# Softmax division in one VectorE piece, row-wise loads for four heads, shared masks, interleaved last products: attention and two gated MLPs on one core

## The chip, the cores and the metric

The kernel runs on one core of a Trainium2 chip. The metric is the device time of one execution, in microseconds (us). Engines are named as in the profile: PE is TensorE, DVE is VectorE, ACT is ScalarE, POOL is GpSimd, SP is SyncE, which here issues every DMA.

## What is computed

Three layers follow each other, all in float32. `q`, `k`, `v` are [4, 8, 576, 64] (batch, head, position, depth).

```python
scores = scale * np.matmul(q, k.transpose(0, 1, 3, 2))
rel = pos[:, None] - pos[None, :]
mask_plain = (rel >= 0) & (rel < 32)
mask_dil = (rel >= 0) & (rel < 128) & (rel % 4 == 0)
# heads 0..3 use mask_plain, heads 4..7 mask_dil
scores = np.where(masks[None], scores, -1e9)
attn = np.exp(scores - np.max(scores, axis=-1, keepdims=True))
attn = attn / (np.sum(attn, axis=-1, keepdims=True) + 1e-9)
x = np.matmul(attn, v)                       # then rows of 512: 2304 x 512
# first MLP: rms norm, then
xn = x / np.sqrt(np.mean(x * x, -1, keepdims=True) + 1e-6) * rms_g
g = xn @ w_gate
y = (g * sigmoid(g) * (xn @ w_val)) @ w_out  # 512 -> 1536 -> 512
# second MLP
out = (sigmoid(y @ w2_gate) * (y @ w2_val)) @ w2_out
```

## The kernel before

**Attention.** Two heads make a pair `hp` (0 and 1 plain, 2 and 3 dilated), so that 128 partitions are full. Both masks leave a window of 96 keys for 64 queries (the dilated heads are sorted by position modulo 4 first), so a pair of one batch is nine blocks, in three groups of three. There are 4 x 4 x 3 = 48 groups. `attn_group` makes one: 12 small score matmuls on PE (L982), mask and row maximum on DVE (L994, three instructions), `exp` with its sum on ACT (L1000, three), `sum + 1e-9` and reciprocal on DVE (L1007, L1008), the division as three multiplications (L1013 on POOL, by choice of the planner L1017 on DVE), three transposes on PE (L1027), their eviction on ACT (L1032), 12 value matmuls on PE (L1040), and an eviction into `xT` (L1052, L1060).

**How q and k come in.** Batch 0 goes through `first_qk`: whole rows of 256 bytes are loaded (L797) and PE turns them (L834, four operations of four transposes for a pair). The other twelve pairs go through `attn_load`: eight DMAs of 128-byte runs into `kraw` and `qraw` (L941), which have one buffer each, and two 32x32 transposes on DVE (L955). Values come through `values_of` (L894 for dilated pairs, L904 and L912 for plain ones), those of batch 0's dilated heads through `first_v` (into `xT`).

**First MLP.** The 2304 rows are six chunks `c` of 384. `x_norm(c)` squares `xT` on ACT (L1090), adds the four 128-row blocks on POOL for c > 0 (L1098, three additions), sums over partitions on PE (L1106), makes 1/sqrt by Newton steps (on DVE for c = 0; on POOL for c > 0, L1140 to L1144), spreads it (L1147, L1163), scales (L1186) and splits each value into a high and a low fp32r part (ACT or DVE L599/L601, POOL L603 or DVE L606). `mlp_step` then runs 12 + 12 matmuls of 384 columns (L1401) and `y_group` 12 more (L1481) for each of 12 blocks `f` of the hidden size; pass 0 takes `f` 0 to 5 for all chunks, pass 1 the rest. Chunk 0 needs ten groups of batch 0; chunk 1 needs ten more: two of batch 0, six of batch 1's dilated pairs and one of each of its plain pairs. The weights come as 64-bit words, are packed on ACT and DVE (L567 to L576) and split in the same way.

**Second MLP.** It works on blocks in seven products instead of eight (`unit`, `half`, L1709; `y_products`, L1632): a product is six matmuls of 288 columns, three for each of two `u`. Its input for a `u` is `hop`, seven high and low pairs, the last made by DVE, ACT and POOL after the last L1709 product. `y_products` gives 14 closures: seven for output half n = 0, then seven for n = 1. They are handed out between the products of the next `unit`; those of the last batch have no next `unit` and run in a row at the end, followed by transposes and stores (L1662, L1667, L1674).

**Order.** `Line` is a list scheduler that runs while the program is built: every `add` gives an operation an engine (or several to choose from), an estimated cost, what it reads and writes, its tiles and a due time. `emit` always takes the operation that can begin first; among operations that wait for a busy engine the smallest due time wins. An alternative engine has a penalty from `PARAMS`. Every engine's program, SP's DMA issues too, is in the order that this leaves. PE's products of the second MLP keep the order in which they were added (key `PE order`).

Of the kernel before, what the change touches and what calls it, by code (L numbers as in the profile page):

```python
# [8 lines left out]
F32 = mybir.dt.float32  # L9
# [6 lines left out]
NEG = -1.0e30  # L16
# [9 lines left out]
    "late": 0, "fill_share": -1.497, "fill_max": 6, "gather": 1.257, "w0_hi": 12.903,  # L26
    "w0_lo": 18.633, "h0_hi": 0.97, "h0_lo": -0.008, "x0_hi": 0.055, "x0_lo": 0.49, "ahead": 2,
    "todo0": 261.292, "todo1": 2.598, "todo2": 1.388, "todo3": 21.487, "xb_zero": 1.369,
    "stay": 0.055, "phase": 1.6, "fill_from": 6.083, "fill_gap": -7.771, "margin": 894.801,
    "wait": 1.635, "w_sq": 1.999, "w_hi": 1.306, "w_lo": 0.0, "x_hi": 5.948, "x_lo": 0.127,  # L30
    "h_hi": 13.236, "h_lo": 0.0, "qk": 0.148, "norm": 0.496, "pts": 11.821, "o": 0.0,
    "snap": 2.101, "h_ahead": 10.497, "h2_ahead": 7.278, "evac": 4.529, "holds": (6, 6),
    "norm_act": 8.92, "slack": 0.0, "share_v": 0.6, "share_p": 0.33, "cold": 1.7, "low": 0,
    "high": 0.39, "recip": 0.3, "rel1": 72.061, "span1": -5.933, "rel2": 16.991, "span2": 0.874,
    "ys": 0.545, "ts": 14.649, "cross": 0.06, "same": 0.04, "dma_lat": 1.7, "dma_rate": 330000.0,
# [3 lines left out]
    "ld_b": -50.429, "ld_v": -48.262, "ld_c": -52.06, "ld_d": -2.674, "lead": -0.197,  # L39
    "xdue": 16.042, "wdue": -1.702, "wslope": 2.797, "wload": -154.451, "wload_step": -3.584,  # L40
    "warm_n": 36, "warm_t": -0.367, "warm_dt": -0.481, "warm_c": 19, "warm_m": 5,
    "warm_late": -1.242, "warm_due": 26.914, "mask_cost": 0.18, "exp_cost": 0.36, "s_cost": 0.546,
# [302 lines left out]
def attention_then_two_gated_mlps(  # L345
# [145 lines left out]
    def build_masks(kinds, due):  # L491

        base = masks["p1"][:, 0]

# [1498 lines left out]
```

## Time and profile before

| | us |
|---|---|
| median of 3 runs | 1003.61 (1000.10 to 1006.71) |
| the profiled execution | 1002.46 |
| its span, first to last instruction | 1000.7 |

The profiled execution has 1.8 us outside its span. The profile gives the busy time of each engine, the granted clock of PE as a share of its full 2.4 GHz, the chain of work that ended last, groups of instructions by line, and what each engine waited for. In rows by stretch the figures are the stretch, its length, then busy us of each engine with the number of its instructions in brackets. A busy PE is busy at its granted clock, so a stretch at 0.7 holds less work than one at 1.0.

### The profile page before, as it was taken

How to read it: one execution, taken by the hardware profiler on the slowest of the kernel's cores; microseconds unless marked ns; L12 is line 12 of the kernel's file. 1: busy time of each engine (PE TensorE's matmuls, PEld its weight loads, DVE VectorE, ACT ScalarE, POOL GpSimd, SP SyncE). 2: the span in 40 equal slices, each digit the busy share in tenths (PEclk: the TensorE clock that was granted, in tenths of full speed). 3: DMA queues.
4: the chain of work that ended last, by engine and by line, in shares of the span. 5: the costliest groups of instructions: out<-in, count | busy, mean ns of one | idle time of the engine just before them, and what ended most of it. 6: DMA issues, size and time to landing. Idle time of an engine off the chain costs nothing.

```text
span 1000.7 us, 20034 instructions
## 1 busy us (share of the span) xinstructions
PE 974.8 (97%) x7096; PEld 943.4 (94%) x7096; DVE 709.3 (71%) x1699; ACT 485.9 (49%) x1336; POOL 332.8 (33%) x512
## 2 busy tenths in 40 slices
PE   7989899999999999999999999999999999999997
PEld 6768799999999999999999999999999999999996
DVE  5687997776884877641322579778987689887775
ACT  5875656664432643322222355657673446444432
POOL 4556865443540100002220124445440017441210
PEclk8779799999999999999999999999999999999999
DMA  9949788594887688965654355545275464548633
GB/s 195 183 102 224 161 222 233 154 250 147 274 297 266 212 302 257 342 217 189 221 197 141 108 168 185 208 170 194 83 270 183 162 221 148 173 143 239 178 81 75
DMA packets 213252, 194.53 MB, mean 194 GB/s; under 512 B 137312, under 2 KB 178848, under 8 KB 213152
## 3 DMA queue, kind: packets, MB, share of 16 engines
q1 hardware_dynamic: 213152, 193.25, 63.1%
q8 instruction: 56, 0.92, 0.4%
q14 instruction: 44, 0.36, 0.1%
HBM read 129.50 MB, written 63.70 MB: 193 GB/s over the span
## 4 chain that ended last, share of the span: by engine, by line
PE 87%; DVE 4%; DMA 3%; SPq 2%; ACT 1%; POOL 1%; issue 1%; ACTq 0%; DVEq 0%; POOLq 0%
PE g L1401 14%; PE y L1481 14%; PE v L1401 14%; PE y L1632 13%; PE att L1709 11%; PE v L1709 5%; PE y L1709 5%; PE g L1709 4%; PE att L982 3%; PE att L1040 2%; SPq L797 1%; DMA xT<-in_v_dram 1%; PE att L1027 1%; DMA out_dram<-ob 1%; PE y L1040 0%
## 5 line engine op out<-in xcount | busy, mean ns | idle before, releaser
L1401 PE MATMUL g<-xo,w 128*128 128x384 f32 x864 | 166.6, 340 | 0.4 <-POOL xo L603 0.4
L1481 PE MATMUL y<-h,wo 128*128 128x384 f32 x864 | 166.4, 338 | 0.0
L1401 PE MATMUL v<-xo,w 128*128 128x384 f32 x864 | 163.3, 336 | 0.7 <-DVE t L1449 0.7
L1401 PEld LDWEIGHTS g<-xo,w 128*128 128x128 f32 x864 | 152.5, 191 | 1.7 <-POOL xo L603 1.0
L1401 PEld LDWEIGHTS v<-xo,w 128*128 128x128 f32 x864 | 149.9, 188 | 2.2 <-DVE t L1449 1.1
L1481 PEld LDWEIGHTS y<-h,wo 128*128 128x128 f32 x864 | 149.5, 188 | 1.4
L599 ACT CAST h<-t 128x384 fp32r<-128x384 f32 (+1 forms) x140 | 66.2, 475 | 103.0 <-DVE t L1449 83.7
L1449 DVE TENSOR_TENSOR t<-t,v 128x384 f32<-128x384 f32 x72 | 39.5, 549 | 82.8 <-PE v L1401 77.8
L603 POOL TENSOR_TENSOR h<-t,h 128x288 fp32r<-128x288 f32 (+1 forms) x45 | 43.6, 970 | 153.1 <-ACT h L599 149.7
L1581 DVE SCALAR_TENSOR_TENSOR pt<-y,pt 128x288 f32<-128x288 f32 x133 | 59.8, 451 | 29.5 <-PE y L1632 28.5
L606 DVE TENSOR_TENSOR h<-t,h 128x384 fp32r<-128x384 f32 (+1 forms) x95 | 56.6, 598 | 24.7 <-ACT h L599 23.5
L1632 PE MATMUL y<-h,wo 128*128 128x288 f32 x399 | 72.1, 295 | 0.3 <-ACT h L599 0.2
L1735 ACT ACTIVATE t<-t 128x288 f32<-128x288 f32 x72 | 31.9, 444 | 73.1 <-DVE t L1726 73.0
L1013 POOL TENSOR_SCALAR pr<-pr,rs 128x96 f32<-128x96 f32 x134 | 51.0, 395 | 46.8 <-DVE rs L1008 37.2
L567 ACT ACTIVATE wz<-wst 128x512 f32<-128x512 f32 x72 | 47.8, 669 | 32.6 <-DMA z<-wz 21.1
L1632 PEld LDWEIGHTS y<-h,wo 128*128 128x128 f32 x399 | 59.3, 188 | 1.1 <-ACT h L599 0.5
L1000 ACT ACTIVATE pr<-pr,nmx 128x96 f32<-128x96 f32 x144 | 52.2, 365 | 12.9 <-DVE nmx L994 12.7
L603 POOL TENSOR_TENSOR w<-wz,w 128x256 fp32r<-128x256 f32 x40 | 32.9, 831 | 73.7 <-ACT w L599 73.7
L576 DVE SCALAR_TENSOR_TENSOR wz<-wst,wz 128x512 int32<-128x512 int32 x72 | 54.7, 763 | 0.8
L570 DVE TENSOR_SCALAR wz<-wz 128x512 int32<-128x512 int32 x72 | 35.2, 493 | 26.8 <-ACT wz L567 25.9
L573 DVE SCALAR_TENSOR_TENSOR wz<-wst,wz 128x512 int32<-128x512 int32 x72 | 53.2, 742 | 1.1
L1270 DVE TENSOR_TENSOR t<-t,t 128x288 f32<-128x288 f32 x82 | 49.7, 608 | 4.2 <-POOL x L603 1.2
(220 smaller groups left out, 2019.9 us busy)
## 6 DMA issues: line engine op xcount, KB each, us to landing
z<-wz SPq DMA_DIRECT2D x54, 256.0 KB, 5.7
xo<-xs SPq DMA_DIRECT2D x23, 576.0 KB, 5.8
wst<-in_moe_w_gate_dram SPq DMA_DIRECT2D x24, 512.0 KB, 6.5
wst<-in_moe_w_val_dram SPq DMA_DIRECT2D x24, 512.0 KB, 5.0
wst<-in_moe_w_out_dram SPq DMA_DIRECT2D x24, 512.0 KB, 6.3
xs<-xs SPq DMA_DIRECT2D x21, 576.0 KB, 2.9
wst<-xs SPq DMA_DIRECT2D x18, 576.0 KB, 4.2
x<-xo SPq DMA_DIRECT2D x24, 384.0 KB, 4.5
```

The source lines that it names most:

```text
L573: add("DVE", Shared(0.595), lambda: nc.vector.scalar_tensor_tensor(out=z.t, in0=top(), scalar=-0x80000000, in1=z.t, op0=ALU.bitwise_and, o ...
L576: add("DVE", Shared(0.595), lambda: nc.vector.scalar_tensor_tensor(out=z.t, in0=low(), scalar=29, in1=z.t, op0=ALU.logical_shift_right, op ...
L599: add("ACT", act(n), lambda: nc.scalar.copy(out=hi(), in_=src()), reads=reads, writes=[key] + [order] * bool(order), tiles=tiles + [dst], ...
L603: add("PL", pool(n), lambda: nc.gpsimd.tensor_tensor(out=lo(), in0=src(), in1=hi().bitcast(F32), op=ALU.subtract), reads=reads, writes=[ke ...
L606: other=(kind + "_lo", "DVE", dves(n), lambda: nc.vector.tensor_tensor(out=lo(), in0=src(), in1=hi().bitcast(F32), op=ALU.subtract)))
L1000: add("ACT", PARAMS["exp_cost"], lambda u=u: nc.scalar.activation(out=pr.t[:, u], in_=pr.t[:, u], func=ACTF.Exp, bias=nmx.t[:, u:u + 1], s ...
L1013: add("PL", Shared(0.305), lambda u=u: nc.gpsimd.tensor_scalar(out=pr.t[:, u], in0=pr.t[:, u], scalar1=rs.t[:, u:u + 1], scalar2=1.0, op0= ...
L1401: nc.tensor.matmul(out=bank.t, lhsT=w[:, l, cols], rhs=x, start=kk == order[0] and n == 0, stop=kk == order[-1] and n == 2)
L1481: nc.tensor.matmul(out=yb.t, lhsT=w.t[:, l, s], rhs=hs[r].t if broad(p, c) else hs[r].t[:, r], start=n == 0 and j == 0, stop=n == HOLDS[p] ...
L1581: add("DVE", dve(T), lambda: nc.vector.scalar_tensor_tensor(out=t.t[:, e, h], in0=bank.t, scalar=0.5, in1=t.t[:, e, h], op0=ALU.mult, op1= ...
L1632: nc.tensor.matmul(out=bank.t, lhsT=w.t[:, u, a, n], rhs=hs[u].t[:, d], start=first and u == 0 and m == 0, stop=u == NF // 2 - 1 and m == ...
L1709: nc.tensor.matmul(out=bank.t, lhsT=l.t[:, a, cols], rhs=r.t[:, d, j], start=first and j == 0 and m == 0, stop=j == 1 and m == 2, skip_gro ...
```

## The change

- **Division.** With `fuse` 99 every group takes the new branch: `divided` issues `sum + 1e-9`, the reciprocal and the three multiplications as one operation on DVE. POOL and ACT have no part in it. (`whole_norm` is 0, so that branch is not built.)
- **Whole rows.** `by_pe` is 2: the first two pairs of batch 1 that are met, its dilated pairs (1, 2) and (1, 3), use `first_qk` with `start=False`, staged in the ring `xo` of four buffers, and PE turns them; their values still come through `values_of`. (`few` is 0: `dilated_values` is not used.)
- **Masks.** Five masks of three blocks become six masks of one block, by bound.
- **Row sums.** With `early_sum` the additions for c > 0 run into block 2, in the order 3, 0, 1, and may run on DVE.
- **Last products.** With `mixed` the 14 closures of the last batch run in the order 0, 7, 1, 8, 2, 3, ... 13; the banks are kept by half and name.
- **Due times and penalties.** Nearly all numbers of `PARAMS` are others. `fast` 1 leaves the Newton steps of c > 0 on POOL as they were. `packed` stays 0.

```diff
-    "high": 0.39, "recip": 0.3, "rel1": 72.061, "span1": -5.933, "rel2": 16.991, "span2": 0.874,
+    "wait": 1.628, "w_sq": 0.142, "w_hi": 10.229, "w_lo": 0.083, "x_hi": 16.209, "x_lo": 0.682,
...
-    "hi3": 58.56, "lo4": 66.519, "hi4": 99.279, "lo5": 125.255, "hi5": 121.604, "ld_a": -59.069,
-    "ld_b": -50.429, "ld_v": -48.262, "ld_c": -52.06, "ld_d": -2.674, "lead": -0.197,
+    "lo4": 75.925, "hi4": 97.447, "lo5": 103.804, "hi5": 68.022, "ld_a": -47.059, "ld_b": -40.139,
+    "ld_v": -42.85, "ld_c": -37.834, "ld_d": -2.595, "lead": 0.175, "xdue": 11.352, "wdue": 2.621,
...
+    "pk": -0.353, "pk_act": -0.974, "pk_pl": 12.322, "few": 0, "sg": -4.518, "early_sum": 1,
+    "sq_add": 0.555, "xdue1": 0.715, "fast": 1, "fuse": 99, "mixed": 1, "whole_norm": 0,
...
-        add("PL", 1.0, band, writes=["band"], due=due)
-        for n, (key, bounds) in enumerate(kinds):
...
+        add("PL", 1.0, band, writes=[("mask", None)], due=due)
+        for n, b in enumerate((0, 16, 32, 48, -16)):
+            m = masks[b]
+            add("DVE", 0.2, lambda m=m: nc.vector.tensor_copy(out=m, in_=base),
+                reads=[("mask", None)], writes=[("mask", b)], due=due + n)
...
+        def divided():
+            recip()
+            for u in range(G):
+                nc.vector.tensor_scalar(
+                    out=pr.t[:, u], in0=pr.t[:, u], scalar1=rs.t[:, u:u + 1], scalar2=None,
+                    op0=ALU.mult)
+
+        if n < PARAMS["fuse"]:
+            add("DVE", Shared(PARAMS["recip"] + 0.34), divided, writes=[("e", gk, u) for u in range(G)],
+                tiles=[pr, rs], due=due + 1.25)
...
+        into = KK_FIRST[0] if PARAMS["early_sum"] else 0
         if c:
-            for kk in range(1, KD):
+            for kk in KK_FIRST[1:] if into else range(1, KD):
                 add("PL", pool(T1), lambda kk=kk: nc.gpsimd.tensor_tensor(
-                    out=sq.t[:, 0], in0=sq.t[:, 0], in1=sq.t[:, kk], op=ALU.add),
-                    reads=[x for x in keys if x[2] == kk], writes=[x for x in keys if x[2] == 0],
-                    tiles=[sq], due=due)
+                    out=sq.t[:, into], in0=sq.t[:, into], in1=sq.t[:, kk], op=ALU.add),
+                    reads=[x for x in keys if x[2] == kk], writes=[x for x in keys if x[2] == into],
+                    tiles=[sq], due=due, other=("sq_add", "DVE", dves(T1),
+                    lambda kk=kk: nc.vector.tensor_tensor(
+                    out=sq.t[:, into], in0=sq.t[:, into], in1=sq.t[:, kk], op=ALU.add)))
...
-                        banks[key] = new("ps", tag, [P, T], F32, 2 if tag == "att" else 1)
+                        banks[n, key] = new("ps", tag, [P, T], F32, 2 if tag == "att" else 1)
...
-                    first_qk(*g[:2], (("at", "kraw", RAWS), ("at", "qraw", RAWS)), at, at, False)
+                    home = (("sb", "xo", NX),) * 2
+                    first_qk(*g[:2], home, at, at, False)
...
+        if PARAMS["mixed"]:
+            extra = [extra[i] for i in (0, 7, 1, 8, 2, 3, 4, 5, 6, 9, 10, 11, 12, 13)]
         for _, fn in extra:
             at += fn(at)
```

## Rows read from the trace of the kernel before

**Rows 1.** Busy us by stretch: length, PE, PEld, DVE, ACT, POOL; clock; DMA share, GB/s

```profile
11.60:30.00 18.40, 14.53 (x149) 11.59 (x149) 12.34 (x61) 13.29 (x52) 8.69 (x19) 0.71 0.99 197
30.00:45.00 15.00, 14.94 (x169) 12.02 (x171) 8.09 (x40) 11.68 (x41) 6.62 (x19) 0.68 1.06 179
45.00:61.40 16.40, 12.36 (x142) 9.07 (x137) 14.01 (x71) 12.87 (x50) 6.58 (x18) 0.76 0.55 138
61.40:111.80 50.40, 48.86 (x430) 42.50 (x429) 40.55 (x123) 34.88 (x122) 35.94 (x59) 0.94 0.75 175
111.80:125.30 13.50, 10.79 (x86) 9.42 (x86) 12.78 (x43) 8.04 (x29) 11.29 (x25) 0.62 0.68 152
125.30:280.00 154.70, 154.40 (x1298) 143.76 (x1297) 120.68 (x353) 88.23 (x276) 78.90 (x156) 1.00 0.77 214
280.00:979.40 699.40, 697.49 (x4706) 695.68 (x4705) 483.49 (x974) 308.77 (x756) 175.53 (x187) 1.00 0.59 198
979.40:1000.70 21.30, 14.38 (x97) 12.55 (x95) 11.27 (x26) 4.11 (x10) 2.39 (x3) 0.96 0.27 57
```

**Rows 2.** Chain of waits, 62 to 150 us: start, us, what, instructions

```profile
95.00 0.64 PE att L982 x12
95.65 0.50 PE att L1040 x12
...
100.30 0.33 PE att L1027 x3
...
103.55 2.08 PE g L1401 x12
```

**Rows 3.** Timeline of PE, 0 to 140 us: start, us, what, shapes, count

```profile
109.50 2.33 PE L1481 MATMUL y<-h,wo 128*128 128x384 f32 x12
...
121.39 4.01 PE L1401 MATMUL g<-xo,w 128*128 128x384 f32 x12
```

**Rows 4.** Groups of PE instructions, 111.7 to 125.3 us: count, busy us, mean ns

```profile
L982 PE MATMUL att<-kT,qT 64*64 64x96 f32 x36 | 3.4, 368 | 0.5 <-DVE ms L1122 0.5
L1040 PE MATMUL att<-pts,v 96*64 96x64 f32 x24 | 1.5, 276 | 0.0
```

**Rows 5.** Timeline of SP's queue, 0 to 120 us: start, us, what, count

```profile
35.45 3.49 SPq L941 DMA_DIRECT2D kraw<-in_k_dram  x4
...
82.36 5.02 SPq L941 DMA_DIRECT2D kraw<-in_k_dram  x4
```

**Rows 6.** Timeline of POOL, 0 to 125 us

```profile
5.56 0.28 POOL L524 MEMSET mask_p<- 64x32 f32 x2
...
102.99 1.14 POOL L1013 TENSOR_SCALAR pr<-pr,rs 128x96 f32<-128x96 f32 x3
...
107.98 2.38 POOL L1098 TENSOR_TENSOR pt<-pt 128x384 f32<-128x384 f32 x2
...
111.75 1.45 POOL L1098 TENSOR_TENSOR pt<-pt 128x384 f32<-128x384 f32 x1
```

**Rows 7.** Chain of waits, 0 to 62 us

```profile
40.05 0.25 PE y L834 x4
```

**Rows 8.** Groups of DVE instructions, 60 to 120 us

```profile
L570 DVE TENSOR_SCALAR wz<-wz 128x512 int32<-128x512 int32 x10 | 5.9, 596 | 3.0 <-ACT wz L567 3.0
...
L1007 DVE TENSOR_SCALAR rs<-rs 128x3 f32<-128x3 f32 x12 | 3.3, 274 | 1.2 <-ACT pr L1000 1.2
```

**Rows 9.** Groups of DVE instructions, 120 to 280 us

```profile
L1007 DVE TENSOR_SCALAR rs<-rs 128x3 f32<-128x3 f32 x23 | 5.1, 221 | 4.1 <-ACT pr L1000 4.1
...
L1017 DVE TENSOR_SCALAR pr<-pr,rs 128x96 f32<-128x96 f32 x7 | 1.9, 282 | 0.2
```

**Rows 10.** Chain of waits, 960 to 1001 us

```profile
978.63 0.81 PE y L1709 x6
...
984.35 2.22 PE y L1632 x14
...
991.45 2.42 PE y L1632 x18
```

More of the change, by code (lines that the diff above doesn't have):

```diff
@@ L25 @@
 PARAMS = {
[L26 to L31, printed above, removed]
@@ L47 @@
-    "turns": 2, "raw0": 0, "sign": 1, "packed": 0, "pk": 0.869, "pk_act": -1.179, "pk_pl": 4.504,
-    "sg": 0.0,
+    "late": 0, "fill_share": -1.979, "fill_max": 6, "gather": 1.675, "w0_hi": 28.354,
+    "w0_lo": 12.639, "h0_hi": 9.993, "h0_lo": 0.526, "x0_hi": 0.211, "x0_lo": 1.621, "ahead": 2,
+    "todo0": 152.278, "todo1": 1.414, "todo2": -1.035, "todo3": 8.412, "xb_zero": -89.067,
+    "stay": 0.59, "phase": 1.6, "fill_from": 12.103, "fill_gap": -6.912, "margin": 510.725,
+    "wait": 1.628, "w_sq": 0.142, "w_hi": 10.229, "w_lo": 0.083, "x_hi": 16.209, "x_lo": 0.682,
@@ new lines @@
+    "h_hi": 10.394, "h_lo": 0.089, "qk": 0.068, "norm": 1.75, "pts": 12.096, "o": 0.661,
+    "snap": 1.157, "h_ahead": 31.842, "h2_ahead": 36.261, "evac": -0.905, "holds": (6, 6),
+    "norm_act": 24.671, "slack": 0.0, "share_v": 0.6, "share_p": 0.33, "cold": 1.7, "low": 0,
+    "high": 0.39, "recip": 0.3, "rel1": 46.586, "span1": -52.882, "rel2": 28.252, "span2": 0.857,
+    "ys": 4.918, "ts": 11.109, "cross": 0.06, "same": 0.04, "dma_lat": 1.7, "dma_rate": 330000.0,
[3 rows of a table added]
+    "ld_v": -42.85, "ld_c": -37.834, "ld_d": -2.595, "lead": 0.175, "xdue": 11.352, "wdue": 2.621,
@@ L489, in constants, with build_masks @@
             writes=["gam"], due=-4)
-    def build_masks(kinds, due):
-        base = masks["p1"][:, 0]
+    def build_masks(due):
+        base = masks[None]
         def band():
@@ L895, in dilated_windows @@
                     out=vt.t[p0:p0 + n, j], in_=vr[r, t0:t0 + n]),
-                    rows(n * n_heads, 4 * D), writes=[key], tiles=[vt], due=due + 0.12 * j)
+                    rows(n * n_heads, 4 * D), writes=[key], tiles=[vt], due=due + 0.12 * j, cost=0.58)
                 vkeys[j].append(key)
@@ L918, in plain_windows, with dilated_values @@
         return vkeys
-    def values_of(b, hp, due):
+    def dilated_values(b, due):
+        vt = new("at", "vd", [WIN, NB, HP, D], F32, 1)
+        pad = ("v pad", b, HP // 2)
+        add("PL", 0.3, lambda: nc.gpsimd.memset(vt.t[0:32, 0], 0.0), writes=[pad], tiles=[vt],
+            due=due)
+        vkeys = dilated_windows(vt, b, HP, HP, due)
+        vkeys[0].append(pad)
+        return vt, vkeys
+    together = {}
+    def values_of(b, hp, due):
+        if hp >= HP // 2 and PARAMS["few"]:
+            if b not in together:
+                together[b] = dilated_values(b, due)
+            vt, vkeys = together[b]
+            heads[b, hp] += (vt, 2 * hp - HP, vkeys)
+            return
         vt = new("at", "v", [WIN, NB, 2, D])
@@ L1108, in sums @@
                                  stop=last and t == TT - 1)
-        order = [0] if c else KK_FIRST
+        order = [into] if c else KK_FIRST
         for n, kk in enumerate(order):
```

105 lines of the change are left out of this document (52 added, 53 removed), and 4 rows, old and new, of the table PARAMS.

## The prediction, made before the changed kernel was run

> **What bounds the kernel now.** I read the page first (busy time, the 40 slices, the chain that ended last), then busy time by stretch, then for each stretch that loses time the chain of waits and the timelines of the engines in it. From 280 to 979.4 us PE is busy for 697.49 of 699.40 us at a granted clock of 1.00, which is the full 2.4 GHz, and from 125.3 to 280 for 154.40 of 154.70 [rows 1]. Nothing that this change does to DVE, ACT or POOL can shorten those 854 us; it can only lengthen them. What can be won lies in three places.
>
> *The front*, to 61.4 us, where chunk 0's first MLP product starts. From 11.6 us, when the first q and k have landed, PE is busy for 14.53 + 14.94 + 12.36 = 41.8 of 49.8 us, at 0.68 to 0.76 of the clock, a mix of its two levels, 1.2 and 2.4 GHz, and to 45 us the DMA engines are as good as full (0.99 and 1.06) [rows 1].
>
> *The gate of chunk 1.* Chunk 0's last product block starts at 109.50 and takes 2.33; the first of chunk 1 starts at 121.39 [rows 3]. In these 9.6 us PE does attention only: 36 score matmuls and 24 value matmuls [rows 4], at the full clock 3 x 0.64 and 2 x 0.50, and three transposes, 0.33, together 3.25 us [rows 2]. So 6.3 us are lost, and the clock falls to 0.62 over the stretch [rows 1]: the first block of chunk 1 takes 4.01 us instead of 2.08 [rows 2, 3], 1.9 more. That is 8.2 us.
>
> *The end.* The last product of the last unit ends at 979.44. The 14 products behind it are 84 matmuls; a run of 18 takes 2.42 us, so they are 11.3 us of work, and they end at 993.87, 14.4 us later [rows 10]. 3.1 us are lost, all before 984.35: from there PE runs without a wait, 71 matmuls in 9.5 us, so that only 13, or 1.7 us, were done in the 4.9 us before. PE waited for the high and low parts of the last `hop`.
>
> **The change part by part.** *Whole rows.* Today four pairs of batch 1 pass one after the other through the single `kraw` and `qraw`, from the first load at 35.45 to the fourth at 82.36 [rows 5]: three steps of 15.6 us. The first two pairs leave this line, so the two plain pairs that chunk 1 also waits for can be loaded some 31 us earlier, and so can every pair behind them. SP issues two DMAs of q and k for such a pair instead of eight; the weights queued behind them go out sooner. In exchange PE turns them: eight operations of 0.25 [rows 7], 2.0 us. They cost nothing if they fall into the 4.0 us that PE idles between 45 and 61.4 [rows 1], and 2.0 if not; I take 1.0. Their eight evictions replace four DVE transposes and go to ACT, which has 3.5 us free there and 15.5 in the next stretch [rows 1]: nothing. With that cover gone they are at most 8 x 0.6 = 4.8 us of ACT, priced by the widest elementwise DVE row [rows 8]. There is one new wait: the staging ring `xo` also holds chunk 0's normed input, whose transposes of the root (L1163) cannot be issued until these rows are turned, and all MLP products stand behind them on PE. Their turns take 2.0 us and have the whole front, so between 0 and 2 us; I take 0.
>
> *Early row sums.* At the gate POOL adds from 107.98 to 113.20: two additions of 1.19, other work, and the third [rows 6]. In the new order two of the three need no block of the plain pairs that comes last, so one of 1.19 is left: 4.0 us less before the 8.2 us of row sums, Newton steps and spread that follow until 121.39 and that stay as they are.
>
> *The division.* At the gate the three multiplications hold POOL for 1.14 us [rows 6]; three on DVE are 3 x 0.28 = 0.85 [rows 9], without a queue behind POOL's splits: 0.3 us or more for each group.
>
> Together these three move chunk 1's normed input by far more than the 9.6 us that it is late; the load is then not what comes last, but the scores, DVE and ACT of ten groups. I take 7.0 of the 8.2 us, since the row sums and the spread of the root (a few small matmuls with no row at the full clock) remain: between 0 and 8.2. What is late next? The later chunks ask for their groups at the same distance as before and lose 0.3 us today in 155 [rows 1], with their loads 31 us less early. I see no second gate.
>
> *DVE's load.* From 60 us on 35 groups pass [rows 8, 9], 105 multiplications; 7 are on DVE already [rows 9], so 98 x 0.282 = 27.6 us come to it. Between 61.4 and 280 it is busy for 40.55 + 12.78 + 120.68 = 174.0 of 218.6 us [rows 1]; it would be 201.6, in 211.6 us if the gate's 7 are saved: 95%. That is what the fullest stretch today shows (12.78 of 13.50 [rows 1]). So it just fits: I take 0, and price the other case below. In the price POOL counts too: a TENSOR_SCALAR of three columns (L1007) takes 0.274 in the stretch to 120 us, where POOL is busy 71%, and 0.221 from there to 280, where it is 51% [rows 1, 8, 9], so each DVE instruction of this kind pays some 0.1 us for POOL's work, and POOL loses 98 x 0.38 = 37 us of it [rows 6].
>
> The Trainium skill, page "SBUF — State Buffer", section "Who interferes with whom", has a rule that speaks against the change: a VectorE instruction that can use two ports, `tensor_scalar` among them, and a GpSimd instruction lock each other out for the whole instruction. By that rule the division would wait behind POOL's splits; the L1007 rows agree in their direction. By the rule's worst case the sum would be that of the slow rival below, by the rows' mean it is the one here.
>
> *Masks.* The last mask is done at 5.84 us [rows 6], before the first turn at 11.6: 0. With that cover gone, less than one POOL instruction of 0.28.
>
> *Last products.* Products 7 and 8 need the same `hop` parts as 0 and 1, and fill 12 matmuls, 1.6 us, into the 3.2 us that PE lacks before 984.35. The rest still waits. I take 1.6; from 0 to 3.1.
>
> *Order in the front.* `first_v`'s due time is now ahead of two pairs' q and k. That helps the value matmuls and delays scores, on DMA engines that are full; the division shortens each group a little. With PE idle for 8.0 us in all from 11.6 to 61.4 [rows 1] I take 0, from -5 to +3.
>
> The sum against the profiled execution: 1002.46 - 7.0 - 1.6 + 1.0 = 994.9, say 994.6 with the 0.3 of a division at the gate. The median of the runs shown is 1003.61, 1.15 above that execution; the runs spread more than that, so I leave the sum as it is.
>
> **The rivals.**
>
> *The front gets shorter too.* Values earlier, no POOL in the division, and PE's turns in its own gaps: if half of the 8.0 idle us come back, 994.6 - 4.0 = 990.6. For it: PE waits there, it does not lack work. Against it: DMA is full to 45 us and the same bytes must come.
>
> *The gate stays.* The chain of 8.2 us behind the last row sum is untouched, and new due times could put other work ahead of chunk 1's groups. Then 994.6 + 7.0 = 1001.6. For it: from 61.4 to 111.8 PE is busy for 48.86 of 50.40 us [rows 1], so attention that comes early pushes chunk 0 back. Against it: such a push loses nothing, since PE's work is the same.
>
> *DVE becomes the bound (the other side).* If the first multiplication of each group waits for half a POOL instruction of 1.19 us, 35 groups cost 21 us more: 222.6 us of DVE, which at 95% take 234 instead of 211.6. That is 22.7 us: 1017. It ends above 1% slower once the wait is over 0.47 us a group (0.95 x (211.6 + 18) = 218.1, less 201.6, over 35). Against it: the rows' mean is near 0.1 for one instruction, and a split that DVE does today can go to the freed POOL.
>
> **How the numbers follow.** Forecast, 994.6, own range 991 to 999: chance 0.45. Shorter front, 990.6: 0.25. Gate stays, 1001.6: 0.20. DVE the bound, 1017: 0.10. A measurement of this kernel can tell about 1% from no change: below 992.4 or above 1012.5 against the profiled execution. Faster: nearly all of the second case and a third of the first, 0.40. Slower: the last case and a little for effects of the many new due times, 0.12. Same: 0.48. The range from 985 to 1004 takes in the first three cases with the bounds of their terms and leaves out the last.
>
> **What would show it.** Right: the first block of chunk 1 follows chunk 0's last within 2 us, takes 2.1 to 2.4 us, and PE's clock is near 1.0 from about 65 us; the two `kraw` loads for batch 1 start before 60; DVE is busy for over 90% from 61 to 280 with PE still above 99% from 125; 14 products at the end take about 12.8 us. Wrong: a PE wait of several us before 125 on DVE (masks, root) or on `xo`; DVE's TENSOR_SCALARs of 96 columns at 0.5 us or more; or the first MLP product after 61.4 us.

## The result, and the profile after

| | before | after |
|---|---|---|
| median | 1003.61 us | 1011.03 us |
| its runs | 999.33 to 1008.57 | 1008.88 to 1014.09 |
| span of the profiled execution | 1000.7 us | 1009.1 us |

The ratio is 1.0071, 95% interval 1.0051 to 1.0091: slower by 7.4 us, where 994.6 was forecast and the range ended at 1004.

Busy time by stretch of the kernel after, with the columns of [rows 1] and its edges (the edge at 979.40 moved to 987.80, the end of the last unit here, and the end of the span to 1009.10):

```profile
11.60:30.00 18.40, 13.64 (x118) 10.55 (x116) 12.91 (x45) 12.93 (x44) 6.33 (x9) 0.50 0.95 201
30.00:45.00 15.00, 14.04 (x155) 12.01 (x156) 11.21 (x63) 11.58 (x46) 1.68 (x4) 0.73 1.01 181
45.00:61.40 16.40, 13.29 (x208) 10.98 (x203) 15.06 (x81) 14.46 (x61) 1.36 (x5) 1.00 0.80 171
61.40:111.80 50.40, 44.89 (x399) 39.20 (x401) 44.57 (x148) 34.22 (x119) 23.85 (x27) 0.90 0.68 174
111.80:125.30 13.50, 10.79 (x114) 9.78 (x110) 13.09 (x52) 9.96 (x40) 9.62 (x22) 0.93 0.53 132
125.30:280.00 154.70, 150.31 (x1285) 140.29 (x1284) 125.17 (x400) 86.92 (x280) 57.04 (x101) 0.99 0.72 195
280.00:987.80 707.80, 704.96 (x4739) 701.57 (x4738) 456.69 (x856) 310.01 (x762) 294.72 (x308) 1.00 0.59 199
987.80:1009.10 21.30, 13.69 (x97) 12.44 (x95) 10.84 (x23) 3.92 (x10) 5.07 (x6) 0.96 0.26 56
```

To see where time is lost, add PE's idle time (length less busy) and what the clock took (busy times one less the clock) in each stretch, for [rows 1] and for this table:

| stretch | before | after |
|---|---|---|
| 11.6 to 61.4 | 19.9 | 19.4 |
| 61.4 to 111.8 | 4.5 | 10.0 |
| 111.8 to 125.3 | 6.8 | 3.5 |
| 125.3 to 280 | 0.3 | 5.9 |

The sum goes from 31.5 to 38.8 us: 7.3 of the 8.4 us by which the span grew. Such a sum places the loss, but only to a few us: taken the same way, the profiled execution of a_tt below, whose span is 3.2 us shorter than that of the kernel after, comes to 42.1. The stretch that I wanted to shorten did get better by 3.3. The two beside it, which I had as nearly full and safe, lost 5.5 and 5.6. From 61.4 to 160 us DVE is busy for 91.26 of 98.60 us (before 80.96), POOL for 43.98 (before 67.92). What PE waited for in that time, in the kernel after (us in total, times, longest):

```profile
PE y L1201 <- DVE rb L1185: 4.3, 1, 4.3
PE att L1061 <- DVE nmx L1006: 3.9, 5, 1.6
PE att L994 <- ACT xT L1094: 1.4, 3, 0.8
PE att L1074 <- ACT pts L1066: 0.9, 2, 0.7
PE att L994 <- DVE qT L967: 0.9, 1, 0.9
PE att L1201 <- DVE nmx L1006: 0.8, 1, 0.8
...
```

9.9 of these 12.2 us end with DVE: the spread root of chunk 0 (`rb`), the masks' row maxima (`nmx`), a turned q. The division itself stands on the chain of the kernel after, beside POOL's additions (L1134, the row sums):

```profile
106.06 2.96 POOL L1134 TENSOR_TENSOR pt<-pt 128x384 f32<-128x384 f32 x3 [1.58 <-ACT pt L1125]
107.07 2.02 DVE pr L1025 x2
```

The first row is POOL's timeline, the second the chain: two multiplications take 2.02 us, where one alone takes 0.21 (below).

### The profile page after: what moved, and what is told of

It reads as the page before. It is cut to its first block, busy times and chain, and to the rows that moved or that the text cites. A ratio compares the mean times of both kernels' runs of the same rounds, so it can differ in the third digit from the quotient of the medians.

```text
span 1009.1 us, 20109 instructions
## 1 busy us (share of the span) xinstructions
PE 972.4 (96%) x7128; PEld 943.4 (93%) x7128; DVE 695.3 (69%) x1676; ACT 488.4 (48%) x1364; POOL 406.8 (40%) x509
## 4 chain that ended last, share of the span: by engine, by line
PE 77%; DVE 8%; DMA 7%; SPq 3%; ACT 2%; issue 2%; POOL 1%; ACTq 0%; DVEq 0%; POOLq 0%
PE y L1519 13%; PE g L1439 13%; PE v L1439 13%; PE y L1670 12%; PE att L1747 10%; PE v L1747 5%; PE y L1747 5%; PE g L1747 4%; DVE pr L1025 1%; DMA wz<-z 1%; DVE wz L567 1%; DMA v<-in_v_dram 1%; DMA xo<-in_q_dram 1%; SPq L888 1%; DMA pt<-in_k_dram 1%
## 5 line engine op out<-in xcount | busy, mean ns | idle before, releaser
L597 POOL TENSOR_TENSOR h<-t,h 128x384 fp32r<-128x384 f32 (+1 forms) x124 | 122.6, 990 | 266.0 <-ACT h L593 246.9
L1519 PE MATMUL y<-h,wo 128*128 128x384 f32 x864 | 168.9, 339 | 0.4 <-DVE h L600 0.4
L1619 DVE SCALAR_TENSOR_TENSOR pt<-y,pt 128x288 f32<-128x288 f32 x133 | 59.7, 450 | 27.6 <-PE y L1670 27.5
L570 DVE SCALAR_TENSOR_TENSOR wz<-wst,wz 128x512 int32<-128x512 int32 x72 | 58.3, 815 | 1.0
L597 POOL TENSOR_TENSOR x<-t,x 128x288 fp32r<-128x288 f32 x36 | 31.6, 881 | 67.2 <-ACT x L593 56.6
L561 ACT ACTIVATE wz<-wst 128x512 f32<-128x512 f32 x72 | 47.2, 670 | 21.3 <-DMA z<-wz 13.8
L564 DVE TENSOR_SCALAR wz<-wz 128x512 int32<-128x512 int32 x72 | 40.2, 562 | 23.0 <-ACT wz L561 22.7
L567 DVE SCALAR_TENSOR_TENSOR wz<-wst,wz 128x512 int32<-128x512 int32 x72 | 55.0, 766 | 0.9
L1478 ACT ACTIVATE t<-g 128x384 f32<-128x384 f32 x36 | 17.7, 492 | 74.2 <-PE g L1439 74.2
L1308 DVE TENSOR_TENSOR t<-t,t 128x288 f32<-128x288 f32 x82 | 47.8, 583 | 8.4 <-POOL h L597 4.2
L1747 PE MATMUL att<-xo,w 128*128 128x288 f32 x336 | 50.5, 296 | 0.7 <-ACT t L1758 0.7
```

The lines of the kernel that those rows point to most:

```text
L561: add("ACT", 0.65, lambda: nc.scalar.activation(out=z.t.bitcast(F32), in_=top().bitcast(F32), func=ACTF.Abs, scale=REBIAS), reads=[("wst", ...
L567: add("DVE", Shared(0.595), lambda: nc.vector.scalar_tensor_tensor(out=z.t, in0=top(), scalar=-0x80000000, in1=z.t, op0=ALU.bitwise_and, o ...
L570: add("DVE", Shared(0.595), lambda: nc.vector.scalar_tensor_tensor(out=z.t, in0=low(), scalar=29, in1=z.t, op0=ALU.logical_shift_right, op ...
L597: add("PL", pool(n), lambda: nc.gpsimd.tensor_tensor(out=lo(), in0=src(), in1=hi().bitcast(F32), op=ALU.subtract), reads=reads, writes=[ke ...
L1308: add("DVE", dves(n), lambda: nc.vector.tensor_tensor(out=dst(), in0=a(), in1=c(), op=ALU.subtract), reads=reads, writes=writes, tiles=til ...
L1519: nc.tensor.matmul(out=yb.t, lhsT=w.t[:, l, s], rhs=hs[r].t if broad(p, c) else hs[r].t[:, r], start=n == 0 and j == 0, stop=n == HOLDS[p] ...
```

## The experiments

Two theories stood at the outset. A: the division loads DVE, and that makes the loss. B: the new due times make it, above all the order of the first loads. Later A is split in two: A1, a TENSOR_SCALAR on DVE stands still while POOL works; A2, DVE has too much work in whatever form.

All medians stand against runs of the kernel before on the same chip; its medians were 1002.0 to 1003.7 us. Runs of one kernel spread over up to 13 us, so differences under about 0.3% tell nothing. "Before" and "after" are the two kernels; "old" and "new" are their due times and penalties.

| kernel | due times | parts | median us | ratio, 95% interval |
|---|---|---|---|---|
| before | old | none | 1002.0 to 1003.7 | 1 |
| b_mixed | old | last products | 1002.85 | 1.0005 (0.9985 to 1.0026) |
| b_early_mixed | old | early sums, last products | 1001.74 | 0.9985 (0.9961 to 1.0009) |
| b_div_dve | old | multiplications on DVE, order kept | 1008.19 | 1.0053 (1.0027 to 1.0079) |
| b_rows | old | whole rows | 1014.88 | 1.0114 (1.0083 to 1.0145) |
| s_all | old | all | 1012.62 | 1.0074 (1.0041 to 1.0108) |
| p_only | new | none | 1015.87 | 1.0114 (1.0091 to 1.0136) |
| a_by0 | new | all but whole rows | 1021.44 | 1.0180 (1.0157 to 1.0203) |
| a_fuse0 | new | all but the division | 1008.45 | 1.0056 (1.0036 to 1.0076) |
| after | new | all | 1011.03 | 1.0071 (1.0051 to 1.0091) |

**The division alone, and the division undone.** In the kernel before the three POOL multiplications are issued on DVE at the same places; in the kernel after those of DVE are issued on POOL. No other instruction moves.

```diff
-            add("PL", Shared(0.305), lambda u=u: nc.gpsimd.tensor_scalar(
+            add("PL", Shared(0.305), lambda u=u: nc.vector.tensor_scalar(
```

> The kernel before, with its order of work unchanged, but all 144 multiplications of the division issued on DVE at the place in the program where POOL's stood. Theory A (DVE's load makes the loss): DVE gets some 134 x 0.28 = 37 us to 280 us, PE waits appear between 60 and 160, and the time rises by 4 to 9 us, to 1008 to 1013. Theory B (the new due times and the order of the first loads make the loss, the division is free or a gain): within 2 us of 1003.6, and the three-column instructions of DVE get shorter.

> The changed kernel, with its order of work unchanged, but the multiplications of the division issued on POOL. Theory A: DVE is freed of 41 us to 280 us, the PE waits from 120 to 160 (5 us) shrink and the time falls by 4 to 7 us, to 1004 to 1007. Theory B: no gain; every group waits for POOL's three times 0.39 and the time is 1010 to 1014.

Measured: b_div_dve 1008.19, slower by 0.53%. a_div_pool 1009.29, ratio 1.0045 (1.0024 to 1.0067) to before; a gain of 0.26% on the kernel after, with intervals that overlap. The division costs some 5 us on the old order, but taking it back to POOL does not repair the new one, although DVE's busy time from 61.4 to 160 us falls from 91.26 to 74.40. POOL then has these multiplications to do (67.71 us busy in the same time), and PE's longest waits still end with DVE: 3.9 us for `rb`, 3.3 for `nmx`. So this run does not tell what the division on DVE is worth in the new order; a_tt below does.

**The due times alone, and all parts on the old due times.** p_only is the kernel after with `fuse`, `by_pe`, `early_sum` and `mixed` at 0; s_all has the numbers of the kernel before and the four parts.

> The changed kernel's due times and penalties, but none of the four parts that can be switched: division as before by the planner's choice, batch 1 through the single buffers, row sums into block 0, last products in their old order (the masks by bound stay). Theory A: the loss goes with the division, so at most 1005. Theory B: the loss is here, 1009 to 1013, with the first MLP product near 67 us as in the changed kernel.

> The old due times and penalties with all four parts: division in one DVE piece, two pairs as whole rows, early row sums, last products interleaved. Theory A: DVE is full from 40 to 160 us as in the changed kernel, 1007 to 1013. Theory B: 1001 or less, with the first MLP product near 61 us.

Measured: 1015.87 and 1012.62. Both are slower than before. The new numbers without the parts for which they were found cost 1.1%, and the parts without the new numbers 0.7%. An effect of a part is thus only defined beside the others: all parts together cost the same on the old numbers (1.0074) as on the new (1.0071), so the new numbers, 1.1% alone, change nothing that can be told beside the parts.

**The order of the first loads.** In the kernel after, the values of batch 0's dilated heads are issued before the q and k of its other pairs. SP's queue in the kernel after, some of its rows, those between left out:

```profile
13.96 2.00 SPq L888 DMA_DIRECT2D xT<-in_v_dram  x4
...
20.05 3.44 SPq L791 DMA_DIRECT2D pt<-in_k_dram  x1
```

The k of pair (0,0) is issued at 20.05; its load takes 9.15 us of the chain of waits, and PE turns it at 29.3. The granted clock from 11.6 to 30 us is 0.50, the lower of the two levels throughout, where it was 0.71 [rows 1]. a_loads puts the due times of two of these loads back in their old order, though not at their old values:

```diff
-    "ld_b": -40.139, "ld_c": -37.834,
+    "ld_b": -44.139, "ld_c": -45.834,
```

> The changed kernel with two due times alone put back in their old order: the q and k of batch 0's other pairs (ld_b, ld_c) are again due before the values of its dilated heads (ld_v). Theory B: the turned k of pair (0,0) and those behind it land earlier again, PE's granted clock from 11.6 to 30 us rises from 0.50 towards 0.7, the first g product moves from 67.0 to 61 to 63 us, and the time falls by 4 to 6 us. Theory A: the first product comes at most 2 us earlier, since DVE works for 15 of 16.4 us ahead of it, and the time falls by less than 2 us.

Measured: 1019.39, ratio 1.0173 (1.0141 to 1.0205), the wrong way. The first MLP product does come earlier, 63.3 instead of 67.0 us. But the list scheduler re-orders all that follows, and the 3.9 us that are no longer lost between 61.4 and 80 us come back more than threefold behind 111 us. PE's longest waits in a_loads from 61.4 to 160 us:

```profile
PE att L1201 <- DVE rb L1185: 5.3, 1, 5.3
PE att L1074 <- DVE nmx L1006: 3.9, 1, 3.9
...
```

Since the order behind it is another, a_loads does not show what the late first product costs by itself. Up to 61.4 us the kernel after lost no more than the kernel before.

**DVE freed of other work.** a_words and b_words pack the weights of pass 0 without the third DVE step; they leave out the lowest three bits of those weights.

```diff
-            add("DVE", Shared(0.595), lambda: nc.vector.scalar_tensor_tensor(
+            add("DVE", Shared(0.595), lambda: p and nc.vector.scalar_tensor_tensor(
```

> The changed kernel in the same order on every queue, but the weights of pass 0 are packed without the third DVE step (L570, 0.81 to 0.86 us each in the changed kernel's trace, 16 of them before 120 us and some 8 more behind); this leaves out the lowest three bits of each packed weight word of pass 0. Theory A (DVE's load is what holds the first 350 us back): DVE is freed of 13 to 14 us before 120 us and 5 or more behind it, the sixth g block (at 124.4 in the changed kernel) starts several us earlier, PE's idle time between 111 and 160 us mostly goes, and the time falls by 4 to 8 us, more than the same step saves in the kernel before. Theory B (the order of the first loads and the new due times): the first g product stays at 66 to 68 us and the time falls by less than 3 us.

> The control: the kernel before in the same order, without the same third step for pass 0 (L576, 0.75 to 0.82 us each; the lowest three bits of each packed weight word of pass 0 are left out). If the sixth g block at 121.39 waits for its weights, as the end of the last split at 121.48 suggests, rather than for chunk 1's norm as my prediction had it, it starts 3 us or more earlier and the time falls by 2 to 5 us. If it waits for attention or for the norm, it stays within 1 us of 121.4 and the time falls by less than 1.5 us. By theory A the saving here is smaller than in the changed kernel, whose DVE is fuller; by theory B the two savings are equal within 1.5 us.

Measured: a_words 1007.35, 1.0036 (1.0016 to 1.0056); b_words 1002.40, 1.0000 (0.9978 to 1.0023). The same step of 0.8 us for each weight block, taken away, is worth 3.7 us in the kernel after (its interval, to 1.0056, just meets that of the kernel after, from 1.0051) and nothing that can be told in the kernel before. The block at 124.44 of the kernel after comes at 121.73, that at 121.39 of the kernel before at 119.49. This speaks for a DVE that PE hangs on in the kernel after and not in the kernel before; theory A has a part in it, if not the whole.

**Whole rows.** b_rows has only `by_pe` 2 on the old due times, a_by0 is the kernel after with `by_pe` 0.

> The kernel before with its old due times and the new masks, and of the other parts only the whole rows: pairs (1,2) and (1,3) staged in the ring xo and turned by PE. My prediction had this part as the larger share of 7 us less, 1.0 of it given back by the turns. The kernel with all four parts on the old due times starts chunk 0 at 67.0 instead of 61.5, the one with the division alone at 62.5: if the turns and their evictions in the front are the rest of that delay, this one starts chunk 0 at 64 to 66 us and is 1 to 4 us slower than before. If the loads of batch 1 bound chunk 1's gate, as I had it, it is 4 us or more faster. If neither holds, it stays within 2 us.

> The changed kernel without the whole rows (by_pe 0): all four pairs of batch 1 pass through the one kraw and qraw again. With all parts undone on the new due times PE waited 4.7 us for chunk 1's root and 4.2 us behind it, between 111 and 160 us, and the time was 1015.9. If the whole rows are what takes those waits out of the changed kernel, they come back here, 3 us or more of them, and the time is 1014 to 1018. If the other parts did it, the waits stay below 2 us and the time is at or below 1011, since eight turns and their evictions are gone.

Measured: b_rows 1014.88, slower by 1.1%; a_by0 1021.44, so the same part, added last, is worth 10 us on the new due times. And s_all and em_ts (below) differ in this part alone, with a ratio of 1.0074 for both: beside the other parts on the old numbers it is worth nothing that can be told. The first product of b_rows comes at 63.0 us, only 1.5 later than before. What it loses lies from 125.3 to 160 us, where PE of the kernel before has next to no idle time (0.3 us from there to 280 [rows 1]); there b_rows has

```profile
125.30:160.00 34.70, 28.25 (x218) 25.36 (x215) 24.95 (x82) 16.96 (x58) 16.45 (x35) 0.80 0.85 212
```

6.5 us idle and 5.6 by the clock, 12.1 in all; 4.4 of them it had won from 111.8 to 125.3, and its profiled execution is 8.1 us longer. The longest wait in it, 3.4 us, is one for `xn` (L1225) on DVE, behind this instruction of DVE:

```profile
122.35 2.78 DVE L1020 TENSOR_SCALAR rs<-rs 128x3 f32<-128x3 f32 x1
```

An addition on three columns, 0.16 us elsewhere. POOL in b_rows at that time:

```profile
122.15 1.01 POOL L1135 TENSOR_TENSOR pt<-pt 128x384 f32<-128x384 f32 x1
123.13 1.97 POOL L598 TENSOR_TENSOR xo<-xn,xo 128x384 fp32r<-128x384 f32 x2
```

DVE's addition ends at 125.13, POOL's third instruction at 125.10. That raised a new question: does a DVE instruction stand still while POOL works? The addition and the division of the kernel after show the same. DVE, its timeline (start, us):

```profile
126.14 1.13 DVE L1019 TENSOR_SCALAR rs<-rs 128x3 f32<-128x3 f32 x1
127.52 1.93 DVE L1025 TENSOR_SCALAR pr<-pr,rs 128x96 f32<-128x96 f32 x3
```

and POOL of the same kernel:

```profile
124.56 1.44 POOL L597 TENSOR_TENSOR w<-wz,w 128x256 fp32r<-128x256 f32 x2
125.96 1.28 POOL L597 TENSOR_TENSOR wo<-wz,wo 128x512 fp32r<-128x512 f32 x1
127.20 1.99 POOL L597 TENSOR_TENSOR xo<-xn,xo 128x384 fp32r<-128x384 f32 x2
```

126.14 + 1.13 = 127.27, and POOL's split ends at 127.24. From 61.4 to 280 us a multiplication of the kernel after takes 0.21 us where POOL is idle (80 of 105) and 0.50 where POOL is busy for more than half of it (23).

**The division in another form.** a_tt keeps the order of the kernel after and makes a group's addition and division two TENSOR_TENSORs; rows_tt changes only the addition in b_rows. em_ts is b_early_mixed with the changed kernel's division, em_tt the same with TENSOR_TENSORs.

```diff
-            for u in range(G):
-                nc.vector.tensor_scalar(
-                    out=pr.t[:, u], in0=pr.t[:, u], scalar1=rs.t[:, u:u + 1], scalar2=None,
-                    op0=ALU.mult)
+            nc.vector.tensor_tensor(
+                out=pr.t, in0=pr.t, in1=rs.t.rearrange("p (g o) -> p g o", o=1)
+                .to_broadcast([P, G, WIN]), op=ALU.mult)
```

> The changed kernel in the same order on every queue; the addition of 1e-9 and the three multiplications of a group, TENSOR_SCALARs so far, are TENSOR_TENSORs: one of three columns against a constant tile, one of 288 columns against the spread reciprocals. Theory A1 (a TENSOR_SCALAR stands still while POOL works): the 288-column instruction takes 0.35 to 0.45 us whether POOL is busy or not, the reciprocal's addition never more than 0.25, DVE is freed of 10 us or more between 61 and 280 us, and the time falls by 3 to 6 us, to 1005 to 1008. Theory A2 (DVE has too much work, whatever its form): the new instructions are stretched beside POOL as the old ones were, or what they save (three times 0.21 against some 0.4 us, 35 groups, 8 us of DVE) brings less than 2.5 us.

> The kernel with the old due times and the whole rows alone (b_rows), same order, with the addition of 1e-9 as a TENSOR_TENSOR against a constant tile; its multiplications stay on POOL. Theory A1: the stop of 2.78 us at 122.35 (L1020, while POOL splits until 125.10) goes, PE's wait of 3.4 us behind it shrinks below 1.5, the clock between 125 and 160 us is above 0.9 instead of 0.80, and the time falls by 4 to 9 us from 1014.9. Theory A2: less than 3 us.

> The kernel with the old due times, early row sums, interleaved last products and the one-piece division of the changed kernel: all of its parts but the whole rows. Without the division it took 1001.7 us. The division added 4.8 us to the kernel before in its own order (1008.2): both theories expect 1004 to 1008 here, and PE waits for DVE between 80 and 160 us.

> The same with the division and the addition of 1e-9 as TENSOR_TENSORs. Theory A1: the loss by the division is gone: 998 to 1002, and POOL is freed of its three multiplications of 0.38 us a group without a price on DVE. Theory A2: it lies within 2 us of em_ts.

Measured: a_tt 1004.00, 1.0009 (0.9980 to 1.0038); em_ts 1013.22, 1.0074 (1.0044 to 1.0103), more than either theory had; em_tt 1004.79, 0.9993 (0.9966 to 1.0020); rows_tt 1011.73, 1.0085 (1.0056 to 1.0115). The form gives back 6 to 8 us on both sets of due times (0.62% from after to a_tt, 0.81% from em_ts to em_tt, with intervals that do not overlap in either pair): about all that the kernel after had lost against before. It gives back none of what was forecast to be gained: a_tt is at 1004.0, not 994.6. But A1 as I had put it fell: the form does not matter. In rows_tt the stop of 2.78 us is still there, the addition now begins at 121.48 and ends at 124.26 with POOL's 124.23, PE still waits 3.5 us for `xn`, and the 3 us between the medians have intervals that overlap. DVE in a_tt:

```profile
129.91 1.12 DVE L1021 TENSOR_TENSOR rs<-rs,least 128x3 f32<-128x3 f32 x1
131.28 1.02 DVE L1026 TENSOR_TENSOR pr<-pr,rs 128x288 f32<-128x288 f32 x1
```

and POOL in a_tt:

```profile
129.72 1.30 POOL L599 TENSOR_TENSOR wo<-wz,wo 128x512 fp32r<-128x512 f32 x1
130.96 2.23 POOL L599 TENSOR_TENSOR xo<-xn,xo 128x384 fp32r<-128x384 f32 x2
```

A TENSOR_TENSOR with both inputs in SBUF stands still too (131.03 and 131.02). What differs is that a group has one multiplication that can be caught instead of three, and 0.46 us alone instead of three times 0.21. By the groups of instructions from 61.4 to 280 us, addition, reciprocal and multiplications took 7.1 + 6.2 + 28.8 = 42.1 us in the kernel after and 8.1 + 6.3 + 18.5 = 32.9 in a_tt, and PE's idle time fell from 12.6 to 9.2. How much of the 6 to 8 us is this work saved on DVE, and how much the groups that came late behind a stop, was not told apart.

**The division on ACT.**

```diff
-                    add("PL", Shared(0.305), lambda u=u: nc.gpsimd.tensor_scalar(
+                    add("ACT", 0.28, lambda u=u: nc.scalar.mul(
```

> The kernel with the old due times, early row sums and interleaved last products (1001.7 us with the division on POOL, 1013.2 with it on DVE as three TENSOR_SCALARs, 1004.8 as one TENSOR_TENSOR), with the three multiplications of every group on ACT. From 61 to 280 us ACT was busy for 131 of 219 us in the kernel before, so 105 multiplications of 0.3 to 0.4 us, 31 to 42 us, find room. If the stops between DVE and POOL and the load on these two are the only cost of the division, the time is 996 to 1001. If ACT's queue, in which the exponentials and the evictions stand, becomes late, PE's waits name ACT (pr, pts) and the time is above 1005.

> The changed kernel (new due times, whole rows) with the three multiplications of every group on ACT, planned anew. With them on POOL or DVE by the planner's choice it took 1008.5 us, with one TENSOR_TENSOR on DVE 1004.0. If what the changed kernel loses is the division alone, it comes to 1000 to 1004 here. If the whole rows and the new due times lose time of their own, it stays at 1005 or above, whatever engine divides.

Measured: em_act 1011.07, 1.0075 (1.0048 to 1.0102); a_act 1016.33, 1.0133 (1.0111 to 1.0154). ACT takes 0.37 us for one multiplication. In em_act:

```profile
61.40:111.80 50.40, 49.16 (x421) 42.45 (x421) 38.73 (x138) 43.72 (x155) 25.29 (x31) 0.83 0.72 169
```

ACT is busy for 43.72 of 50.40 us (before 34.88 [rows 1]), the first product comes at 73.1 us and PE waits 2.7 us for a cast of weights on ACT. The loss is not in this stretch alone, and PE's longest wait, 3.5 us between 111 and 160, ends with a row maximum on DVE; that ACT has too little room ahead of chunk 1 is argued, not shown. On the old due times the division costs least where the kernel before has it, for the most part on POOL, which takes the longest of the three for one instruction (0.38 us).

**Last products, and early sums with them.** b_mixed is the kernel before with `extra = [extra[i] for i in (0, 7, 1, 8, 2, 3, 4, 5, 6, 9, ...)]` and banks kept by half; b_early_mixed has `early_sum` too.

> The kernel before with the last 14 products interleaved and nothing else changed. My prediction had 1.6 us less for this part (0 to 3.1). If the low part of the last hop sets the end, wherever the products stand, the gain is below 0.7 us. From the changed kernel's trace, in which that low part moved to POOL and the 14 products took 14.1 instead of 14.4 us, I expect here, with the low part still on DVE, between 1 and 2 us less from the last unit's product to the last product, and a time 0.1 to 0.2% lower, which three rounds can hardly tell from nothing; the rows of the end decide.

> The kernel before with its old due times and the new masks, and only the early row sums and the interleaved last products. The interleaving alone gave 0.46 us between the last unit and the last product and no difference that could be told in the time. My prediction had the early sums as 4.0 us less ahead of chunk 1's root. If chunk 1's root is not what PE waits for in the kernel before, the sums bring nothing: the time stays within 2 us of before, 1002 to 1005. If they matter as I had it, the time is 998 to 1000.

Measured: no difference that can be told in either (table); the 1 to 2 us expected of b_mixed are below what the runs can tell. In b_mixed the last product ends 13.97 us after the last unit's, before 14.43: 0.5 gained. In b_early_mixed the block that I called the gate starts 2.2 us earlier, at 119.21, but the time shows no gain that can be told.

**The division handed back to the planner.** a_fuse0 is the kernel after with `fuse` 0, in an order of its own.

> The changed kernel without the one-piece division (fuse 0): three multiplications that the planner hands to POOL or DVE again, with an order of its own. Theory A (DVE's load makes the loss): DVE is busy for less than 31.5 of 34.7 us from 125 to 160 instead of 33.6, PE's waits for the masks' row maxima (L1006, 2.6 us from 111 to 160) shrink below 1, and the time falls to 1004 to 1008. The rival: the loss lies in the new order as such, and the time stays within 2.5 us of 1011. A third case: POOL's queue, with the low parts that the new penalties send to it, becomes late instead, and the time is above 1013.

Measured 1008.45: 2.6 us better than the kernel after, but with intervals that overlap, and 0.56% slower than before. It lies just above what theory A had and just outside the rival's range, and decides nothing. No version was found that beats the kernel before by more than the runs spread: b_early_mixed, a_tt and em_tt are within 0.2% of it.

## Why the prediction was wrong, step by step

Two steps of the prediction failed. The 7.0 us for the gate rested on a row that was misread, and the row sums ahead of that block ended later than before, not earlier. And "so it just fits: I take 0" for the division on DVE was wrong by 6 to 8 us, as a_tt against after and em_tt against em_ts show. With the second mended (a_tt, 1004.0) the time is that of the kernel before, so none of the gains in the sum came.

**The gate: a misread row.** I took the block at 121.39 [rows 3] for chunk 1's first. Counting `g` blocks in PE's timeline of before (they begin at 61.47, 73.41, 82.14, 92.65, 103.39, 121.39, then 131.68) shows that it is chunk 0's sixth, f = 5. It needs nothing of chunk 1. Chunk 1's spread root only stands ahead of it in PE's queue. The chain of waits of before names what came last, a row that I had not read:

```profile
119.64 0.26 DVE pr L994
...
120.26 0.46 DVE rb L1147
...
120.87 0.87 PE att L1163 x3
121.74 3.66 PE g L1401 x12
```

Ahead of PE's L1163 the chain runs on DVE. POOL's row sums, from which I took 4.0 us, had been added by 113.20. The Newton steps behind them end almost together with DVE's queue, the last at 120.11:

```profile
119.92 0.19 POOL L1144 TENSOR_TENSOR rsy<-rsy,rsa 128x3 f32<-128x3 f32 x1
```

So both had to come earlier. (A third limit is as near: the block's own weights were split on POOL from 120.07 to 121.48.) In b_early_mixed the last addition ends at 111.17, 2.0 us earlier, the chain runs through POOL's Newton steps, and the block comes 2.2 us earlier. In PE's timeline of after:

```profile
122.63 0.51 PE L1061 MATMUL att<-ident,pr 128*96 128x128 f32 x3 [1.63 <-DVE nmx L1006]
123.92 0.87 PE L1201 MATMUL att<-ident,rb 128*128 128x128 f32 x3 [0.78 <-DVE nmx L1006]
124.44 3.48 PE L1439 MATMUL g<-xo,w 128*128 128x384 f32 x12
```

the same block comes 3 us later than before, behind two waits for DVE's masks. The input of the row sums was late too. The loads did come earlier, but chunk 1's last squares on ACT end at 113.59, before at 107.90, and two additions follow them on POOL, not the one that I counted on:

```profile
113.08 0.51 ACT L1125 ACTIVATE pt<-xT 128x384 f32<-128x384 f32 x1
113.97 1.01 POOL L1134 TENSOR_TENSOR pt<-pt 128x384 f32<-128x384 f32 x1
```

The last row sum ends at 114.97, before at 113.20. Why the squares came so late is not shown in full; the last plain pair's values were issued at 102.0 us, before at 96.3, and the stopped division at 107.07 stands on the chain behind them. The stretch itself lost 3.3 us less than before, since the clock fell to 0.93 only; my term was 7.0. And behind it, where I saw no second gate, from 125.3 to 280 us, 5.6 us more were lost.

**DVE just fits: an average over stages.** The sum of 201.6 us from 61.4 to 280 was too high. Measured are 44.57 + 13.09 + 125.17 = 182.8: splits on DVE fell by 8.4 us, as I thought they might, and the packing of weights by 9.8, since less of it fell into this time. Yet my comparison with 95% hid the place: from 61.4 to 160 us DVE is full to 93%, and there PE's waits end with it. The price of one multiplication, 0.282, was right as a mean (0.275) and wrong as a kind of number: it is 0.21 or, beside POOL, 0.50.

**The rival that DVE becomes the bound** had the sign and the mechanism. Its price of 1017 did not come, since the stops were smaller: over 105 multiplications 28.8 - 105 x 0.211 = 6.7 us, and for the 35 additions 7.1 - 35 x 0.16 = 1.5 us, 0.23 us a group in all. I had put the deciding point for a loss over 1% at 0.47. Here the Trainium skill, page "SBUF — State Buffer", section "Who interferes with whom", goes further than the rule I quoted: a VectorE instruction with two SBUF inputs also contends with a GpSimd instruction that reads SBUF, and whoever issues first keeps the shared ports for its whole instruction. The rows of a_tt, two SBUF inputs, agree with it (131.03 against 131.02), and those of the kernel after, a TENSOR_SCALAR, with the rule that I quoted (127.27 against 127.24). I set that rule aside because L1007's mean differed by only 0.05 us. A mean hides this: of the 23 instructions behind 0.221 all but two took under 0.5 us, and those two 0.58 and 0.98.

**The new due times: no term at all.** I gave "a little" to 87 changed numbers of 118. Alone they cost 1.14%, as much as any part. Beside all the parts they cost nothing that can be told (s_all against after), so the missing term is not a cost of theirs that could be added: parts and numbers do not add.

**Whole rows.** The loads did move, if less than 31 us: the third pair's `kraw` load starts at 44.84 instead of 70.16, the fourth's at 70.61 instead of 82.36, so only one of the two starts before 60. The part is worth -10 us on the new due times and +11 on the old ones by itself, against -7.0 + 1.0 in the sum. What b_rows loses lies between 125 and 160 us, where DVE ends PE's waits and one of them stands behind a stop of 2.78 us; that the stop makes the loss was not shown, since rows_tt did not remove it, and how the same part comes to help on the new due times stays open.

**The front.** The first product came at 67.0 us, after 61.4, which I had named as a sign of being wrong. PE stood 4.35 us for chunk 0's root, since the last row sums came at 58.7 instead of 52.9. With the clock (0.50 to 30 us, but 1.00 from 45 on) the front up to 61.4 was still even, 19.4 against 19.9, so the term of 0 held there and the cost appears behind it.

**Last products.** 1.6 us were forecast, from 71 matmuls after 984.35; the rows show 68, so that PE lacked 2.8 us and not 3.2. From the last unit's last product (987.83: its `v` matmuls end at 987.03 in the chain, six of `y` at 0.80 follow) to the last product (1001.14) the kernel after takes 13.31 us, before 14.43: 1.1 gained. The chain of after shows what ate the rest:

```profile
990.12 0.81 DVE pt L1619 x2
990.93 1.02 DVE t L1308
...
992.49 0.81 POOL h L597
```

The interleaved products must be evicted, and their evictions (L1619) stand on DVE ahead of the sum (L1308) that makes the last `hop`; and by the new penalties the low part went to POOL, 0.81 instead of 0.46 us on DVE. The sum itself took 1.02 instead of 0.46 us, beside POOL's splits. Even the 1.1 us do not reach the end of the span, which comes 21.3 us after the last unit in both kernels, for SP issues sixteen stores in a row, and the last stores wait behind them. SP's queue, before and after:

```profile
986.82 9.08 SPq L1690 DMA_DIRECT2D out_dram<-ob  x16
996.00 0.40 SPq L1674 DMA_DIRECT2D out_dram<-wz  x1
995.70 8.54 SPq L1728 DMA_DIRECT2D out_dram<-ob  x16
1004.34 0.40 SPq L1712 DMA_DIRECT2D out_dram<-wz  x1
```

The rows that the first of these last stores (`wz`) writes were ready at 994.92 and at 1002.20, so it waited 1.1 us before and 2.1 after. The masks cost nothing that can be told (b_early_mixed has them); the evictions on ACT were not measured by themselves.

## What to carry to other kernels

Before pricing a gate, count the blocks to know which one it is, follow the chain of waits to the engine that ends last, and look how close behind it the next one ends: here DVE's queue, POOL's Newton steps and a split of weights ended within 1.4 us, so that a gain in one of them can bring little. Work moved to an engine must be summed for the stretch in which PE hangs on that engine, not over the stage, and on DVE its cost is that of instructions beside POOL: here one long instruction for a group was better than three short ones by 6 to 8 us of the kernel. Where a list scheduler makes the order, its due times are a change of their own, and the parts do not add: test a part on both sets, and by leaving it out of the whole as well as by itself.

## What the runs showed of the hardware

In the rows shown above, a TENSOR_SCALAR on DVE, or a TENSOR_TENSOR with both inputs in SBUF, begun while POOL works, ends with an instruction of POOL: 0.16 us become 1.13, and 2.78 beside three of POOL's in a row. A RECIPROCAL, one input in SBUF, is not stopped; in the kernel after it runs beside POOL's splits of 127.20 to 129.19 at its usual 0.18 us:

```profile
127.30 0.18 DVE L1020 RECIPROCAL rs<-rs 128x3 f32<-128x3 f32 x1
```

One that reads a PSUM input is not stopped either; of the kernel after, the first of these runs beside POOL's split of 124.56 and the second with POOL idle:

```profile
124.83 1.39 DVE L1224 SCALAR_TENSOR_TENSOR xn<-xT,gam,att 128x192 f32<-128x192 f32 x4
130.87 1.36 DVE L1224 SCALAR_TENSOR_TENSOR xn<-xT,gam,att 128x192 f32<-128x192 f32 x4
```

POOL pays too: its Newton steps on three columns take 0.19 us, and 0.52 for those begun between 119.67 and 121.48 in the kernel after, while DVE packs weights.
